# Feed-forward blocks as pairs of tiles across batches, behind an exact top-32 attention

## The chip, the cores and the metric

The kernel runs on one core of a Trainium2 chip, in one launch. The metric is device time in microseconds (us). A core has five engines that run their own instruction streams in order: TensorE (PE, matmuls; its weight loads are listed apart as PEld), VectorE (DVE), ScalarE (ACT), GpSimd (POOL) and SyncE (SP), which here only issues DMAs.

## The reference

Eight batches, eight heads, 576 positions, head dimension 64; then a feed-forward part over all 4608 positions with 512 inputs, 2048 hidden units and 512 outputs.

```python
scores = q @ k.T / sqrt(64)                       # per batch and head, 576 x 576
kth    = np.partition(scores, -32)[..., -32]      # the 32nd largest of each row
scores = np.where(scores >= kth, scores, -1e9)
attn   = softmax(scores)
x      = (attn @ v), heads side by side           # (4608, 512)
h      = x @ w_in                                 # (4608, 2048)
g      = np.where(h > 0, h, exp(min(h, 0)) - 1)   # ELU
out    = g @ w_out                                # (4608, 512)
```

All is in float32. The two weight matrices arrive as float64 and are decoded on the chip during the first steps.

## The kernel before

**Steps.** A batch has four query tiles of 128 rows (numbers 0 to 3) and a remainder of 64 rows (number 4, `J` in the code). The heads are taken in pairs. One step is one query tile and one head pair: 128 rows x 576 keys, twice. Two remainders share a step: it takes four heads of 64 rows. So a batch has 4 x 4 + 2 = 18 steps, and the whole kernel 144. The list `steps` fixes their order. Before, batch 0 takes its tiles one by one and then the remainder; every other even batch takes tiles (0,1), then (2,3), then the remainder; an odd batch begins with the remainder and goes on with (0,1) and (2,3). Inside a group such as (0,1) the order is head pair by head pair, and for each head pair tile 0 and then tile 1.

**What a step does.** `scores` (L329) is four fp32 matmuls of 288 columns on PE (eight half-high ones in a remainder step), and ACT copies and scales them (L337). In the profile each fp32 matmul of the program is two instructions. `select` (L349 to L363) finds the 32nd largest value of every row on DVE with four MAX8 and three MATCH_REPLACE8 for each of the two heads: it is almost all of DVE's work. `mask` (L382 to L386) does mask and exponential on ACT. `normalise` (L396 to L403) divides on POOL. `turn` (L422, L423) transposes the weights of the step on PE in nine chunks of 128 and copies them to `et` with ACT. `attend` (L448) multiplies by v, once per group and head pair: 20 matmul instructions of 256 columns for a group of two tiles, 20 of 128 columns for a single tile, and 40 of 64 columns for a remainder step. `finish` (L475) copies the result into `xT`, the input of the feed-forward block to which the tile belongs.

**The order on PE.** Every engine's instructions stay in the order in which the main loop at the end of the kernel writes them. Iteration n writes: the scores of step n+2, the attend of a group that became complete, then four quarters. The selection of step n is spread over the quarters on DVE; mask and normalise are those of step n-1, and the transposes are those of step n-2. At the end of each quarter `feed` may put feed-forward pieces in. `todo` holds loads and transposes of the next batch's k and q, and loads of v, at steps given by `plan`: `load_halves` issues eight DMAs on SP, `start_qk` leads to two transposes on DVE (L283), `load_v` issues four DMAs on SP and two memsets on POOL. A buffer of `kqT` or `vT` (five each) comes free after the last scores or the last attend that use it.

**Feed-forward blocks.** A `Block` holds one, two or three tiles (`slots`). It becomes ready when the attends of all its tiles are done. Then `ffn_pieces` makes 16 hidden pieces and, per tile, four projection pieces. A hidden piece (L523) is four matmuls (eight instructions) of 128 x `slots` columns; ACT makes ReLU twice and an exponential (L533, L536, L538) and mostly a subtraction (L542), and POOL (L493) or DVE (L495) adds the halves. A projection piece (L551) is four matmuls (eight instructions) of 512 columns for one tile. A tile is stored from `osb` by SP.

Before, the first two batches form five single blocks and two pairs; each further two batches form the blocks (0,1), (2,3), (remainders, 0, 1 of the odd batch) and (2,3 of the odd batch): three pairs and a triple. In all there are five singles, eleven pairs and three triples for 36 tiles.

**The planner.** `HIDDEN` and `PROJECT` give each piece a planned cost; a single has 31.8 units in all, a pair 58.0, a triple 85.8. The list `due` holds for each block the step at which it becomes ready and the units of all blocks that were ready before it. `feed` goes on at the lowest rate that any of these due times asks for:

```python
ahead = [(w - fed["sum"]) / (x - fed["at"]) for x, w in due if x > fed["at"]]
if ahead:
    fed["over"] += max(0.0, share * min(ahead))
```

So the work that is at hand is spread up to the next block that is late in coming. Some entries of `due` before: 391.0 units at step 66.5, 650.8 at 102.5, 910.6 at 138.5, 996.4 at 146.5; the sum of all blocks is 1054.4. Pieces that are left when the loop ends are written behind it.

Of the kernel before, what the change touches and what calls it, by code (L numbers as in the profile page):

```python
# [10 lines left out]
FP32 = mybir.dt.float32  # L11
# [5 lines left out]
TAKEN = -1.0e30  # L17
EPS = 1.0e-9
STEEP = 2.0**96
HIDDEN = {1: 1.1, 2: 1.85, 3: 2.7}  # L20
PROJECT = 3.55


# [57 lines left out]
def kernel(  # L81
# [10 lines left out]
    P = nc.NUM_PARTITIONS  # L92
    B, H, S, D = q.shape
    dm, dff = moe_w_in.shape[0], moe_w_in.shape[1] // 2
    J = S // P
    JP = J * P
    R = S - JP
# [2 lines left out]
    NC = dm // P  # L100
    NF = dff // P
    NG = NF // 2
    T = 3 * P
    KEYS, QUERIES = R, R + S
    Q = 32
    NB = S // Q
# [19 lines left out]
    late = {}  # L126
# [342 lines left out]
    def finish(blk, parts, at, cols, src):  # L469
        if blk.xT is None:  # L470
            if blk.slots == 1:
                blk.xT = xpool.tile([P, NC, P], FP32, tag="xT", name="xT")
            else:
                blk.xT = late["x"].tile([P, NC, T], FP32, tag="xT", name="xT")
        nc.scalar.copy(blk.xT[:, at, cols], src)  # L475
# [7 lines left out]
    def close_gates(keep=0, upto=None):  # L483

        while gates:
            put, group, dst, n, apart = gates[0]
            if put > place[0] - keep if upto is None else group > upto:
                return  # L490
            gates.pop(0)
            if apart:
                nc.gpsimd.tensor_tensor(dst, n, dst, ALU.add)  # L493
                continue
            nc.vector.scalar_tensor_tensor(  # L495
                out=dst, in0=n, scalar=-1.0, in1=dst, op0=ALU.add, op1=ALU.add
            )

    def ffn_pieces(blk):
        n_tok = blk.slots * P  # L500
        bank = dm // n_tok
        unit = max(2, bank)

        def hidden(f):
            if f == 0 and blk.number == 0:
                g = early.tile([P, NF, P], FP32, tag="g", name="gT")
                blk.gT = [g[:, 0:NG], g[:, NG:NF]]
            elif f % NG == 0 and blk.number > 0:
                g = late["g"].tile([P, NG, T], FP32, tag="g", name="gT")
                blk.gT.append(g[:])  # L510
            if f % unit == 0:
                if len(gates) > 1:
                    close_gates(upto=gates[0][1])
                if blk.number == 0:
                    n = earlyf.tile([P, 4 * P], FP32, tag="n", name="n")
                else:
                    n = late["f"].tile([P, 2 * T], FP32, tag="n", name="n")
                blk.n = n[:, 0 : unit * n_tok].rearrange("p (f t) -> p f t", f=unit)
            if f % bank == 0:
                ps = ps_f.tile([P, dm], FP32, tag="f", name="hps")  # L520
                blk.h = ps[:, 0 : bank * n_tok].rearrange("p (f t) -> p f t", f=bank)
            for i in range(NC):
                nc.tensor.matmul(  # L523
                    blk.h[:, f % bank, :],
                    w_in[:, i, f * P : (f + 1) * P],
                    blk.xT[:, i, 0:n_tok],
                    start=(i == 0),
                    stop=(i == NC - 1),
                )
            g, end = blk.gT[f // NG], f % NG + 1  # L530
            if end % bank == 0:
                n0 = f % unit + 1 - bank
                nc.scalar.activation(  # L533
                    blk.n[:, n0 : n0 + bank, :], blk.h, AF.Relu, scale=-1.0
                )
                nc.scalar.activation(g[:, end - bank : end, 0:n_tok], blk.h, AF.Relu)  # L536
            if end % unit == 0:
                nc.scalar.activation(blk.n, blk.n, AF.Exp, scale=-1.0)  # L538
                dst = g[:, end - unit : end, 0:n_tok]
                apart = place[0] > 4 * (tight + 3) and blk is not blocks[-1]  # L540
                if apart:
                    nc.scalar.activation(blk.n, blk.n, AF.Copy, bias=-1.0)  # L542
                gates.append((place[0], (blk.number, f + 1 - unit), dst, blk.n, apart))

        def project(s, part):
            close_gates(upto=(blk.number, (part + 1) * NF // 4 - 1))
            if part == 0:
                blk.o = ps_f.tile([P, dm], FP32, tag="f", name="ops")
            step = NF // 4
            for f in range(part * step, (part + 1) * step):  # L550
                nc.tensor.matmul(  # L551
                    blk.o[:],
                    blk.gT[f // NG][:, f % NG, s * P : (s + 1) * P],
                    w_out[:, f, :],
                    start=(f == 0),
                    stop=(f == NF - 1),
                )
            if part == 3:
                o = opool.tile([P, dm], FP32, tag="osb", name="osb")
                nc.scalar.copy(o[:], blk.o[:])  # L560
                for t in blk.tiles[s]:
                    p0 = t.cols.start - s * P
                    nc.sync.dma_start(out[t.rows, :], o[p0 : p0 + t.ql, :])

        part = HIDDEN[blk.slots]
        behind = 2 * NF if blk.number else 0
        return [
            (part, max(behind, NC * (f // 4 + 1)), lambda f=f: hidden(f), blk.number)
            for f in range(NF)
        ] + [  # L570
            (PROJECT, max(behind, NF + (part + 1) * NF // 4),
             lambda s=s, part=part: project(s, part), blk.number)
            for s in range(blk.slots)
            for part in range(4)
        ]

    ffn = []
    steps, first, due = [], {}, []
    blocks, tight = [], 2 * NHP
    for b in range(B):  # L580
        if b % 2 == 0:
            rest = 2 * J
            division = [(0,), (1,), (2,), (3,), (rest,), (4, 5), (6, 7)]
            if b > 0:
                division = [(0, 1), (2, 3), (rest, 4, 5), (6, 7)]
            slots = {}
            for part in division:
                blk = Block(len(blocks), len(part))
                blocks.append(blk)
                slots.update((x, (blk, s)) for s, x in enumerate(part))  # L590
        first[b] = len(steps)
        tiles = []
        for qt in range(J + 1):
            r0 = b * S + (JP if qt == J else qt if b == 0 else qt * P)
            if qt == J:
                (blk, slot), c0, n = slots[rest], (b % 2) * R, R
                rows = slice(r0, r0 + R)
            else:
                (blk, slot), c0, n = slots[(b % 2) * J + qt], 0, P
                rows = slice(r0, r0 + J * (P - 1) + 1, J) if b == 0 else slice(r0, r0 + P)  # L600
            c0 += slot * P
            t = Tile(b, qt, rows, blk, slice(c0, c0 + n))
            blk.left += NHP
            blk.tiles[slot].append(t)
            tiles.append(t)
        order = [(0, 1), (2, 3), (J,)] if b % 2 == 0 else [(J,), (0, 1), (2, 3)]
        if b == 0:
            order[:2] = [(0,), (1,), (2,), (3,)]
        for qts in order:
            for hp in range(NHP // 2 if qts == (J,) else NHP):  # L610
                group = Group([tiles[qt] for qt in qts], hp)
                steps += [Step(tiles[qt], hp, group, i) for i, qt in enumerate(qts)]
            for qt in qts:
                n = len(steps)
                tiles[qt].block.ready = n + 2.0 if n <= tight else n + 2.5
    NS = len(steps)
    total = 0.0
    for blk in sorted(blocks, key=lambda x: x.ready):
        due.append((blk.ready, total))
        total += NF * HIDDEN[blk.slots] + 4 * blk.slots * PROJECT  # L620

    todo = {}

    def at(step, fn, *args):
        todo.setdefault(step, []).append((fn, args))

    for b in range(1, B):
        f = first[b]
        plan = ((7, 5, 2), (5, 3, -2), (3, 1, -2), (1, -1, -3))
        if b % 2 == 1:  # L630
            plan = ((7, 5, 0), (6, 4, -2), (5, 3, -3), (4, 3, -3))
        for hp, (ahead, ready, late_v) in enumerate(plan):
            at(f - ahead, load_halves, b, hp)
            at(f - ready, start_qk, b, hp)
            at(f - late_v, load_v, b, hp)
# [44 lines left out]
    main, rest, other = slice(0, J), slice(J, J + 1), slice(J + 1, 2 * J + 1)  # L680
# [69 lines left out]
```

## Time and profile before

| | |
|---|---|
| time, median of 3 runs | 1633.8 us (1633.7 to 1633.95) |
| the profiled execution's own time | 1633.17 us |
| its span | 1631.4 us |
| granted TensorE clock, mean | 0.988 |
| PE, matmuls | 1569.5 us busy, 8276 instructions |
| PEld, weight loads | 1004.7 us |
| DVE | 1454.4 us, 2980 instructions |
| ACT | 1174.6 us |
| POOL | 711.6 us |
| hidden matmuls, L523 | 2432 instructions: 1408 of 256 columns, 384 of 384, 640 of 128 |
| projection matmuls, L551 | 1152 instructions of 512 columns |

The span runs from the first to the last instruction; 1.8 us of the profiled execution lie around it. Busy times of engines overlap, so they say which engine is loaded, not what the end waits for. Matmul ends are modelled in the profile, and matmuls overlap: the time that a group of matmuls takes from PE is read from its start to the start of the next group, not from its own length.

### The profile page before, as it was taken

The page shows a single profiled execution, that of the slowest core. Times are in us where ns is not written, and L with a number is a line of the kernel's source. Part 1 is how long each engine was busy: PE and PEld are TensorE (multiplying, and loading weights), DVE is VectorE, ACT ScalarE, POOL GpSimd, SP SyncE. Part 2 cuts the span into 40 slices and gives each one's busy share as a digit, 9 for nine tenths or more (in the row PEclk, how much of TensorE's full clock was granted, in tenths as well). Part 3 has the DMA queues.
Part 4 walks back from the last instruction along what each step waited for, and adds up shares of the span by engine and source line. Part 5 has one row for each costly group of instructions (what it writes and reads, how often), then busy time and mean ns, then how long its engine had stood idle before and what let it go on. Part 6 is the DMA issues. An engine that isn't in the chain of part 4 may idle for free.

```text
span 1631.4 us, 25301 instructions
## 1 busy us (share of the span) xinstructions
PE 1569.5 (96%) x8276; PEld 1004.7 (62%) x8276; DVE 1454.4 (89%) x2980; ACT 1174.6 (72%) x2369; POOL 711.6 (44%) x1535
## 2 busy tenths in 40 slices
PE   4789999999999999999999999999999999999999
PEld 2477666766665757555566666655557575755564
DVE  7899999999999999999999699999999599998000
ACT  6987777877776868778577786868668695958521
POOL 4983345444443444444344443535435353534300
PEclk9779999999999999999999999999999999999999
DMA  8521310012100310022000200012100201000000
GB/s 243 187 79 36 65 37 1 7 22 45 43 1 19 54 37 7 7 40 46 23 8 15 55 21 25 1 28 45 36 14 1 43 1 36 1 13 1 7 14 13
DMA packets 188035, 56.17 MB, mean 34 GB/s; under 512 B 178176, under 2 KB 179200, under 8 KB 187904
## 3 DMA queue, kind: packets, MB, share of 16 engines
q1 hardware_dynamic: 186704, 54.26, 14.1%
q8 instruction: 66, 1.08, 0.3%
q14 instruction: 65, 0.53, 0.1%
q10 hardware_dynamic: 1200, 0.30, 0.1%
HBM read 45.09 MB, written 9.44 MB: 33 GB/s over the span
## 4 chain that ended last, share of the span: by engine, by line
PE 74%; ACT 14%; DVE 5%; POOL 3%; issue 1%; SPq 1%; DMA 1%; ACTq 0%; DVEq 0%; POOLq 0%
PE ops L551 29%; PE hps L523 22%; PE avps L448 10%; PE scps L329 7%; PE eps L422 5%; ACT sc L386 3%; DVE wk L356 2%; ACT sc L385 2%; ACT et L423 2%; DVE m L363 2%; ACT n L542 1%; ACT n L533 1%; ACT n L538 1%; ACT gT L536 1%; POOL sc L403 1%
## 5 line engine op out<-in xcount | busy, mean ns | idle before, releaser
L363 DVE MAX8 m<-wk 128x8 f32<-128x576 f32 x864 | 611.2, 751 | 0.3 <-POOL den L384 0.3
L523 PE MATMUL hps<-xT,w_in 128*128 128x256 f32 (+2 forms) x2432 | 542.9, 373 | 0.0
L551 PE MATMUL ops<-w_out,gT 128*128 128x512 f32 x1152 | 522.5, 598 | 0.0
L523 PEld LDWEIGHTS hps<-xT,w_in 128*128 128x128 f32 x2432 | 404.9, 192 | 97.4 <-issue 25.4
L356 DVE MATCH_REPLACE8 wk<-m,wk 128x576 f32<-128x576 f32 x576 | 424.5, 747 | 0.0
L551 PEld LDWEIGHTS ops<-w_out,gT 128*128 128x128 f32 x1152 | 208.6, 190 | 231.7 <-issue 230.6
L396 POOL TENSOR_SCALAR dene<-den 128x2 f32<-128x2 f32 x144 | 32.5, 225 | 693.1 <-ACT sc L386 692.5
L386 ACT ACTIVATE sc<-sc,den 128x576 f32<-128x576 f32 x288 | 223.4, 776 | 66.1 <-POOL den L384 44.4
L385 ACT ACTIVATE sc<-sc,m 128x576 f32<-128x576 f32 x288 | 225.0, 781 | 9.6 <-DVE m L363 9.5
L337 ACT ACTIVATE sc<-scps 128x576 f32<-128x576 f32 x288 | 170.9, 646 | 77.8 <-PE scps L329 77.8
L448 PE MATMUL avps<-et,vT 128*64 128x256 f32 (+2 forms) x2080 | 205.6, 328 | 20.1 <-ACT et L423 19.7
L329 PE MATMUL scps<-kqT 64*128 64x288 f32 (+1 forms) x1280 | 199.9, 443 | 25.1 <-ACT kqT L305 12.6
L349 DVE MAX8 m<-sc 128x8 f32<-128x576 f32 x288 | 202.6, 747 | 20.6 <-ACT sc L337 20.6
L403 POOL TENSOR_SCALAR sc<-sc,rec 128x576 f32<-128x576 f32 x288 | 213.5, 751 | 14.9
L423 ACT COPY et<-eps 128x512 f32<-128x512 f32 x288 | 164.6, 571 | 66.2 <-PE eps L422 66.2
L356 DVE MATCH_REPLACE8 wk<-m,sc 128x576 f32<-128x576 f32 x288 | 212.2, 746 | 0.0
L448 PEld LDWEIGHTS avps<-et,vT 128*64 128x64 f32 x2080 | 128.0, 141 | 101.0 <-ACT et L423 34.2
L422 PEld LDWEIGHTS eps<-ident,sc 128*128 128x128 f32 x1152 | 143.4, 143 | 72.4 <-issue 53.9
L493 POOL TENSOR_TENSOR gT<-n,gT 128x512 f32<-128x512 f32 (+1 forms) x120 | 166.2, 1385 | 38.0 <-ACT n L542 38.0
L422 PE MATMUL eps<-ident,sc 128*128 128x128 f32 x1152 | 174.1, 277 | 0.1
L329 PEld LDWEIGHTS scps<-kqT 64*128 64x128 f32 (+1 forms) x1280 | 107.0, 182 | 102.5 <-issue 46.2
L533 ACT ACTIVATE n<-hps 128x512 f32<-128x512 f32 (+1 forms) x156 | 87.0, 558 | 58.0 <-PE hps L523 57.1
(45 smaller groups left out, 988.5 us busy)
## 6 DMA issues: line engine op xcount, KB each, us to landing
raw<-in_moe_w_in_dram SPq DMA_DIRECT2D x16, 512.0 KB, 4.9
vT<-in_v_dram SPq DMA_DIRECT2D x64, 128.0 KB, 2.4
raw<-in_moe_w_out_dram SPq DMA_DIRECT2D x16, 512.0 KB, 3.8
out_dram<-osb SPq DMA_DIRECT2D x32, 256.0 KB, 2.0
kin<-in_k_dram SPq DMA_DIRECT2D x112, 72.0 KB, 2.4
qin<-in_q_dram SPq DMA_DIRECT2D x112, 72.0 KB, 2.5
kin<-in_k_dram SPq DMA_DIRECT2D x8, 128.0 KB, 4.7
vT<-in_v_dram SPq DMA_DIRECT2D x64, 16.0 KB, 2.2
```

Source lines behind the costliest of these rows:

```text
L329: nc.tensor.matmul(wide[i][rows, half, 0:HS], kq[part, q0 : q0 + u.t.ql], kq[part, k0 : k0 + HS], start=True, stop=True,)
L349: nc.vector.max(found[i], cur[i])
L356: nc.vector.match_replace(wk[i], found[i], cur[i], TAKEN)
L363: nc.vector.max(found[i], cur[i])
L385: nc.scalar.activation(sc, sc, AF.Prelu, scale=-1.0, bias=low, alpha=1.0 / STEEP)
L386: nc.scalar.activation(sc, sc, AF.Exp, scale=-STEEP, bias=gap, accum_out=u.den[:, i : i + 1])
L403: nc.gpsimd.tensor_scalar(u.sc[:, i, :], u.sc[:, i, :], rec[:, i : i + 1], 1.0, ALU.mult, ALU.mult)
L422: nc.tensor.transpose(ps[:, c * P : (c + 1) * P], sc[:, c0 : c0 + P], ident[:])
L423: nc.scalar.copy(g.et[:, chunks, u.at, :], ps[:, 0 : n * P].rearrange("p (c q) -> p c q", c=n),)
L448: nc.tensor.matmul(ps[i * D : (i + 1) * D, cols], vt[:, 2 * J + i if c == J else i * J + c, :], w, start=(c == 0), stop=(c == J),)
L523: nc.tensor.matmul(blk.h[:, f % bank, :], w_in[:, i, f * P : (f + 1) * P], blk.xT[:, i, 0:n_tok], start=(i == 0), stop=(i == NC - 1),)
L551: nc.tensor.matmul(blk.o[:], blk.gT[f // NG][:, f % NG, s * P : (s + 1) * P], w_out[:, f, :], start=(f == 0), stop=(f == NF - 1),)
```

## The change

The blocks are no longer cut inside two batches. The list `ends` holds all tiles in the order in which they become complete (a pair of remainders counts where the odd batch's remainder stands), and is cut into five blocks of one tile and then blocks of two; the last tile is left over as a single block. So that two tiles of a pair come together, a batch whose first tile would complete a pair takes its tiles as (0), (1,2), (3) in place of (0,1), (2,3): these are batches 3, 4 and 7. There are now six singles and fifteen pairs. The largest block has two tiles, so `T` falls from 384 to 256, and with it the sizes of `xT`, `gT` and `n`. A further plan holds for an even batch that begins with one tile (batch 4). Entries of `due` are now 391.0 units at step 62.5 and then 58 more every 8 steps up to 971.0 at 142.5, and 1029.0 at 146.5; the sum is 1060.8.

```diff
-HIDDEN = {1: 1.1, 2: 1.85, 3: 2.7}
+HIDDEN = {1: 1.1, 2: 1.85}
...
-    T = 3 * P
+    T = 2 * P
...
-                    n = late["f"].tile([P, 2 * T], FP32, tag="n", name="n")
+                    n = late["f"].tile([P, 4 * P], FP32, tag="n", name="n")
...
+    orders, ends, division = [], [], []
     for b in range(B):
-        if b % 2 == 0:
-            rest = 2 * J
-            division = [(0,), (1,), (2,), (3,), (rest,), (4, 5), (6, 7)]
-            if b > 0:
-                division = [(0, 1), (2, 3), (rest, 4, 5), (6, 7)]
-            slots = {}
-            for part in division:
-                blk = Block(len(blocks), len(part))
-                blocks.append(blk)
-                slots.update((x, (blk, s)) for s, x in enumerate(part))
+        if b == 0:
+            order = [(0,), (1,), (2,), (3,)]
+        elif (len(ends) + b % 2 - J - 1) % 2 == 0:
+            order = [(0, 1), (2, 3)]
+        else:
+            order = [(0,), (1, 2), (3,)]
+        orders.append([(J,)] + order if b % 2 else order + [(J,)])
+        ends += [(b, qt) for qts in orders[b] for qt in qts if qt < J or b % 2]
+    while ends:
+        n = 1 if len(blocks) <= J else 2
+        blk = Block(len(blocks), len(ends[:n]))
+        blocks.append(blk)
+        division += [(x, (blk, s)) for s, x in enumerate(ends[:n])]
+        del ends[:n]
+    slots = dict(division)
+    for b in range(B):
         first[b] = len(steps)
         tiles = []
         for qt in range(J + 1):
             r0 = b * S + (JP if qt == J else qt if b == 0 else qt * P)
             if qt == J:
-                (blk, slot), c0, n = slots[rest], (b % 2) * R, R
+                (blk, slot), c0, n = slots[b | 1, J], (b % 2) * R, R
...
-                (blk, slot), c0, n = slots[(b % 2) * J + qt], 0, P
+                (blk, slot), c0, n = slots[b, qt], 0, P
...
-        order = [(0, 1), (2, 3), (J,)] if b % 2 == 0 else [(J,), (0, 1), (2, 3)]
-        if b == 0:
-            order[:2] = [(0,), (1,), (2,), (3,)]
-        for qts in order:
+        for qts in orders[b]:
             for hp in range(NHP // 2 if qts == (J,) else NHP):
...
         plan = ((7, 5, 2), (5, 3, -2), (3, 1, -2), (1, -1, -3))
+        if len(orders[b][0]) == 1:
+            plan = ((7, 5, 2), (5, 3, 0), (3, 1, -1), (2, 0, -2))
         if b % 2 == 1:
             plan = ((7, 5, 0), (6, 4, -2), (5, 3, -3), (4, 3, -3))
```

Each entry of `plan` is for one head pair: how many steps before the batch's first step its k and q are loaded, its transposes begin and its v is loaded (a negative number lies behind the first step).

## Prediction

> **What bounds the kernel now.** I read the page first: TensorE is the busiest engine, VectorE the next, and the slices show where each gives out.
>
> ```profile
> PE 1569.5 (96%) x8276; PEld 1004.7 (62%) x8276; DVE 1454.4 (89%) x2980; ACT 1174.6 (72%) x2369; POOL 711.6 (44%) x1535
> PE   4789999999999999999999999999999999999999
> DVE  7899999999999999999999699999999599998000
> ```
>
> PE is full from the fourth slice on; DVE is full until about slice 22, then dips, and has nothing to do in the last three slices, where only feed-forward matmuls are left. A PE that is "9" everywhere can still wait, because its ends are modelled. So I cut the span at three starts of score matmuls in the timeline of PE: the scores of step 32 start at 329.8, of step 72 at 739.2, of step 140 at 1457.9, and PE's last matmul ends at 1627.6. The table of stages (columns: busy time of each engine):
>
> ```profile
> 329.80:739.20 409.40, 401.12 (x2081) 256.88 (x2080) 406.73 (x837) 306.84 (x618) 179.35 (x410) 1.00 0.14 28
> 739.20:1457.90 718.70, 715.78 (x3661) 446.29 (x3660) 680.86 (x1402) 531.14 (x1074) 312.50 (x708) 1.00 0.11 23
> 1457.90:1627.60 169.70, 168.65 (x629) 98.29 (x628) 53.86 (x108) 79.02 (x156) 39.21 (x75) 1.00 0.03 8
> ```
>
> In stage A (40 steps, 10.24 us each) DVE is busy 406.7 of 409.4 us: DVE sets the pace. In stage B (68 steps, 10.57 us each) PE is busy 715.8 of 718.7 and DVE has 38 us of idle: PE sets the pace. Stage C is PE alone. To see PE's real need I price each kind of matmul by the start of its group to the start of the next group, in the timeline of PE:
>
> ```profile
> 134.01 1.31 PE L448 MATMUL avps<-et,vT 128*64 128x128 f32 x20
> 135.25 3.70 PE L551 MATMUL ops<-w_out,gT 128*128 128x512 f32 x8
> 138.79 0.60 PE L422 MATMUL eps<-ident,sc 128*128 128x128 f32 x4
> ...
> 168.77 1.06 PE L523 MATMUL hps<-xT,w_in 128*128 128x128 f32 x8
> 169.66 0.60 PE L422 MATMUL eps<-ident,sc 128*128 128x128 f32 x4
> ...
> 726.02 2.75 PE L523 MATMUL hps<-xT,w_in 128*128 128x384 f32 x8
> 728.60 0.60 PE L422 MATMUL eps<-ident,sc 128*128 128x128 f32 x4
> ...
> 1079.66 2.38 PE L448 MATMUL avps<-et,vT 128*64 128x256 f32 x20
> 1081.97 3.70 PE L551 MATMUL ops<-w_out,gT 128*128 128x512 f32 x8
> ...
> 1572.30 27.79 PE L523 MATMUL hps<-xT,w_in 128*128 128x256 f32 x128
> 1599.93 27.63 PE L551 MATMUL ops<-w_out,gT 128*128 128x512 f32 x64
> ```
>
> Prices: projection (512 columns) 0.43 us each (3.44 for 8 in undisturbed groups); hidden 128 columns 0.111 (0.89 for 8), 256 columns 0.217 (27.79 for 128), 384 columns 0.3225 (2.58 for 8); an attend of 256 columns 2.31, of 128 columns 1.24 (both 20 matmuls), of a remainder group 1.31; a transpose 0.109; the scores of a step 1.17. With the counts that stand between the same scores in the built program's order, stage A needs 264 x 0.43 + 512 x 0.217 + 72 x 0.3225 = 247.8 of feed-forward and 132.7 of attention, 380.5 together: 28.9 us of PE gap in 409.4. Stage B needs 470.2 + 225.7 = 695.9: gap 22.8 in 718.7, or 0.335 us a step. Stage C needs 141.3 + 24.1 = 165.4: gap 4.2. The waits of PE show what the gap in A is:
>
> ```profile
> PE avps L448 <- ACT et L423: 19.7, 26, 2.4
> ```
>
> Most of these lie before 800 us: PE runs ahead of a late DVE, and catches up with the last transposed chunk that ACT still has to copy.
>
> **What moves.** The planner feeds feed-forward work by due times. Before, the first nine blocks (391 of its units) are spread up to step 66.5, since a triple is then the next to be ready; after, the same 391 units are due by step 62.5. From there on both run at nearly the same rate (259.8 units in 36 steps, 7.22 a step; after 58 in 8, 7.25). At the end, before leaves a pair (58 units) behind the last due time, after a single (31.8). So work of about one tile moves from the tail to steps 32 to 72. The order of the two built programs says the same: by step 72 the new kernel has issued 28.6 us more of feed-forward matmuls, and the difference stays between 26 and 29.5 us until step 140.
>
> **What it costs PE in total.** Nine tiles leave triples: 384 hidden matmuls x 0.3225 = 123.8 us become 512 x 0.217 + 128 x 0.111 = 125.3: +1.5. In three batches twelve paired attends become 24 single ones: 24 x 1.24 - 12 x 2.31 = +2.0. Projections, scores and transposes keep their number. Sum +3.5 us.
>
> A rule speaks against this. The Trainium skill, "TensorE: Matmul & The Clock Gate", Part 3, The mechanism, states that a weight load overlaps running matmuls only where the row groups differ. The rows differ from it: a load for `hps` takes 0.190 us, yet hidden matmuls of 128 columns start every 0.111 us, so loads lie under matmuls of the same rows. By the page the 256 added hidden loads and 240 added attend loads would be exposed, 256 x 0.190 + 240 x 0.137 = 81 us, and the kernel would take about 1700 us.
>
> **The stages after.** A: 320 x 0.43 + 640 x 0.217 = 276.5 plus attention 133.0 = 409.5, up 29.0. That is above DVE's 406.7, so the stage becomes like B, where PE needs 10.23 a step and DVE 10.0. I take B's gap, 0.335 x 40 = 13.4: 422.9, against 409.4: **+13.5**. Bounds: the calmest steps of B (1206 to 1248 us, for one) show 0.7 us of gap in four steps, 0.175 a step, giving 7 and +7.1; if nothing of the 28.9 is filled, +29.0. B: 520 x 0.43 + 1136 x 0.217 = 470.1 plus 227.1 = 697.2, **+1.3**. C: 160 x 0.43 + 144 x 0.217 + 128 x 0.111 = 114.3 plus 24.4 = 138.7, against 165.4: **-26.7**. Sum -11.9.
>
> Beside PE, at no cost: ACT's feed-forward work per tile is 9.67 us in a triple (32 x 0.4845 + 8 x 0.846 + 8 x 0.843, over 3) and 9.78 in a pair (16 x 0.5915 + 8 x 0.632 + 8 x 0.630, over 2); twelve more copies of attends add 1.9 us; ACT has 188 us idle in B. If that cover failed it would be 1.9 us. POOL's additions become 32 x 1.277 for 24 x 1.819, 2.8 us less. Twelve more attends can each meet a late ACT copy: ten single ones between 127 and 213 us took 1.58 on average, 0.34 over 1.24, so 4 us at most; but in the new order nearly every attend has a feed-forward piece between it and the transposes it needs, where 24 of 60 had none in A and B. I take 0 and keep -6 (24 bare attends at the mean excess of 0.28 in B's paired ones) to +4.
>
> The new load plan touches batch 4 alone. One load of k and q (eight DMAs on SP), one pair of transposes on DVE and three loads of v (four DMAs on SP and two memsets on POOL each) come one to two steps earlier; their numbers stay. A load of v and its memsets wait for an attend of batch 3, at the nearest one step earlier in the order; behind them stand output stores on SP (one every 14 us at the densest) and the next normalise on POOL. Odd batches of before have the same spacing in B and cost PE nothing there: 0. The scores of the last two head pairs now come one step after their transposes (1.5 us a pair), where before left two or more; a lagging DVE would hold PE by those 1.5 us and a ScalarE copy, some 2 us, twice. No row shows it: -1 to +4, taken as 0, since a stage set by PE leaves DVE ahead.
>
> In the tail the new kernel still covers the last chain: some 65 us of matmuls stand between the last scores and the last transposes; two selections of 9.7 us on DVE, the mask (4 x 0.78 on ACT) and the normalise (about 3 us on POOL) need under 30.
>
> The profiled execution took 1633.17 (span 1631.4, and 1.8 around it), 0.6 under the median 1633.8. 1633.17 - 11.9 = 1621.3; on the median's scale **1621.9**.
>
> **Rivals.** 0.2%, 3.3 us, is about what a measurement here can tell from no change.
> (1) *ACT, not DVE, makes the gap.* Then A keeps 28.9 (+15.5 over my sum), and each of twelve new attends pays the worst bare excess seen, 0.98: +11.8. Net +15.4: **1649, slower**. Place: the attend waits of steps 32 to 72 and of batches 3, 4, 7. It decides from a gap of 0.63 us a step in A (25.3 us). For it: in A the chain of waits runs 23% through ACT and 69% through PE. Against: ACT has nearly the same load per step in A and B (7.7 and 7.8 us), and in B the chain is 95% PE and 4% ACT.
> (2) *The gap is latency that neither grows nor fills:* A 438.4, sum +3.6, **1637**, at the edge between no change and slower.
> (3) *Everything runs as in the calmest steps,* since bare attends are gone: A 416.5, B 709.1, C 142.9, sum -29.2, **1605**. Against: batch starts, with their transposes on DVE, cost B 3.5 and 4.5 us of gap in four steps, twice.
>
> **Chances.** My forecast 0.72; its bounds (A's gap at 7, attends at -6, up to +4 and +4) give 1609 to 1630. Rival 1 0.08, rival 2 0.10, rival 3 0.10. The range 1609 to 1638 takes in rival 2 and leaves out 1 and 3. Faster: 0.72 less 0.03 for its upper end, plus rival 3, is 0.79; no change 0.03 and half of rival 2, 0.08; slower the other half and rival 1, 0.13.
>
> **What would show it.** Right: the scores of steps 32 and 72 some 423 us apart instead of 409, with DVE idle there; steps 72 to 140 unchanged at 10.6; the end beginning with a run of 128 hidden matmuls of 128 columns (14.2 us) and 13.8 of projection; DVE ending some 10 us later than before. Wrong: gaps above 25 us in A, attends waiting on ACT in batches 3 and 4, or a PE wait for transposed keys at step 72.

## The result: 27 us slower; stages A and B lose 55 us, the tail gains 29

The changed kernel takes 1660.77 us (median of 4 runs, 1660.61 to 1661.11) against 1633.75 in the same session: ratio 1.0168, 95% interval 1.0150 to 1.0185. The prediction was 1621.9, with 1638 as its upper end and 0.13 for slower.

The page of the profile after, engines and slices:

```profile
PE 1572.4 (95%) x8772; PEld 1050.6 (63%) x8772; DVE 1453.2 (88%) x2976; ACT 1181.3 (71%) x2385; POOL 721.2 (43%) x1551
PE   4789999999999999999999999999999999999999
DVE  7899999999998899989898599989999779999500
```

The work is what was counted: 8772 matmul instructions are 256 hidden and 240 attend instructions more than 8276. PE looks full as before. But DVE now has dips from slice 13 on: its first operation of a step (L349) waited 55.9 us in all for ScalarE's scores, and 20.6 us in the kernel before. The stages are cut at the same scores as in the prediction (steps 32, 72, 140, end of PE):

```profile
331.60:763.30 431.70, 421.92 (x2233) 274.68 (x2232) 418.23 (x860) 315.45 (x635) 185.32 (x418) 1.00 0.14 28
763.30:1514.60 751.30, 724.31 (x3959) 480.14 (x3958) 677.42 (x1392) 540.18 (x1089) 316.49 (x713) 1.00 0.10 22
1514.60:1654.90 140.30, 140.30 (x677) 90.32 (x676) 43.47 (x87) 69.17 (x140) 38.76 (x79) 1.00 0.03 8
```

Stage A went from 409.4 to 431.7 us (the sum had 422.9), stage B from 718.7 to 751.3 (720.0), stage C from 169.7 to 140.3 (142.9). With 1.8 us lost before step 32 and 0.2 gained behind PE's last matmul that is +27.1, the difference of the spans. The tail did what was forecast, and stage B lost 31 us that the sum did not have. PE's waits in stage B, first of the kernel before and then of the changed one (total, times, longest):

```profile
PE avps L448 <- ACT et L423: 1.8, 2, 1.1
```

```profile
PE avps L448 <- ACT et L423: 27.0, 21, 2.8
```

So attends wait for ScalarE's copy to `et`. (This view counts idle time alone; from start to start, the measure of the table further below, stage B's attends lose 30 us more than before.) One of them, in the timeline of PE and then in that of ACT:

```profile
1311.76 0.60 PE L422 MATMUL eps<-ident,sc 128*128 128x128 f32 x4
1312.20 1.89 PE L523 MATMUL hps<-xT,w_in 128*128 128x256 f32 x8
1314.02 1.24 PE L329 MATMUL scps<-kqT 64*128 64x288 f32 x8
1315.19 0.65 PE L448 MATMUL avps<-et,vT 128*64 128x256 f32 x2
1316.80 2.37 PE L448 MATMUL avps<-et,vT 128*64 128x256 f32 x18 [0.96 <-ACT et L423]
```

```profile
1313.26 0.78 ACT L386 ACTIVATE sc<-sc,den 128x576 f32<-128x576 f32 x1
1313.94 0.19 ACT L386 ACTIVATION_READ_ACCUMULATOR sc<-sc,den 128x1 f32 x1
1314.03 0.58 ACT L533 ACTIVATE n<-hps 128x512 f32<-128x512 f32 x1
1314.51 0.59 ACT L536 ACTIVATE gT<-hps 128x512 f32<-128x512 f32 x1
1314.99 0.63 ACT L538 ACTIVATE n<-n 128x512 f32<-128x512 f32 x1
1315.65 0.63 ACT L542 ACTIVATE n<-n 128x512 f32<-128x512 f32 x1
1316.18 0.57 ACT L423 COPY et<-eps 128x512 f32<-128x512 f32 x1
```

PE goes on from the transposes at 1312.2. A hidden piece (1.82 us to the next start) and the scores (1.17) lie between them and the attend, so PE's side has its cover. The copy starts 4 us after the transposes, because four operations for a finished bank of hidden units (two ReLU, exponential, subtraction) stand ahead of it in ScalarE's queue. The attend's first two matmuls use an earlier copy and go; the other eighteen wait.

In the program order, an iteration has four quarters, and the last transposes with their copy stand between the third feed and the fourth. A pair's PSUM bank holds two hidden pieces, and a piece is fed about once a quarter; so banks end either in quarters 1 and 3 or in 2 and 4. A bank that ends in quarter 3 stands ahead of the copy, one in quarter 4 behind it. In stage B the kernel before ended 4, 29, 5 and 31 banks in quarters 1 to 4, the changed kernel 34, 2, 34 and 2 (a hidden piece of a triple fills a bank alone). Its plan repeats every 8 steps (58 units at 7.25 a step), so each block falls into the same phase.

### The profile page after: what moved, and what is told of

Same layout as the page of the kernel before. It is cut to its first block, busy times and chain, and to the rows that moved or that the text cites. A ratio compares the mean times of both kernels' runs of the same rounds, so it can differ in the third digit from the quotient of the medians.

```text
span 1658.5 us, 26360 instructions
## 1 busy us (share of the span) xinstructions
PE 1572.4 (95%) x8772; PEld 1050.6 (63%) x8772; DVE 1453.2 (88%) x2976; ACT 1181.3 (71%) x2385; POOL 721.2 (43%) x1551
## 4 chain that ended last, share of the span: by engine, by line
PE 66%; ACT 24%; DVE 7%; issue 1%; POOL 1%; DMA 0%; ACTq 0%; SPq 0%; DVEq 0%; POOLq 0%
PE ops L551 29%; PE hps L523 15%; PE avps L448 10%; PE scps L329 6%; ACT sc L386 5%; PE eps L422 5%; ACT sc L385 4%; DVE wk L356 3%; ACT n L542 3%; ACT et L423 3%; ACT n L533 3%; ACT n L538 3%; ACT gT L536 2%; DVE m L363 2%; ACT sc L337 1%
## 5 line engine op out<-in xcount | busy, mean ns | idle before, releaser
L523 PE MATMUL hps<-xT,w_in 128*128 128x256 f32 (+1 forms) x2688 | 547.7, 354 | 0.0
L523 PEld LDWEIGHTS hps<-xT,w_in 128*128 128x128 f32 x2688 | 444.0, 193 | 62.3 <-issue 20.8
L349 DVE MAX8 m<-sc 128x8 f32<-128x576 f32 x288 | 202.6, 745 | 56.8 <-ACT sc L337 55.9
L493 POOL TENSOR_TENSOR gT<-n,gT 128x512 f32<-128x512 f32 x136 | 173.6, 1277 | 145.9 <-ACT n L542 145.9
L448 PEld LDWEIGHTS avps<-et,vT 128*64 128x64 f32 x2320 | 136.2, 141 | 128.5 <-ACT et L423 61.9
L533 ACT ACTIVATE n<-hps 128x512 f32<-128x512 f32 x144 | 84.7, 588 | 85.2 <-PE hps L523 85.1
```

The source lines that it names most:

```text
L349: nc.vector.max(found[i], cur[i])
L448: nc.tensor.matmul(ps[i * D : (i + 1) * D, cols], vt[:, 2 * J + i if c == J else i * J + c, :], w, start=(c == 0), stop=(c == J),)
L523: nc.tensor.matmul(blk.h[:, f % bank, :], w_in[:, i, f * P : (f + 1) * P], blk.xT[:, i, 0:n_tok], start=(i == 0), stop=(i == NC - 1),)
```

## Experiments

Theory P (place of the bank in ScalarE's queue) stood against S (single-tile groups and their extra attends) and L (ScalarE overloaded while a pair's hidden pieces run). The kernel before took 1633.4 to 1633.7 us beside these runs.

**e1_due_quarter**

```diff
-                tiles[qt].block.ready = n + 2.0 if n <= tight else n + 2.5
+                tiles[qt].block.ready = n + 2.0 if n <= tight else n + 2.75
```

> The changed kernel, with one constant of the planner altered: a block counts as ready 2.75 steps behind its last step and not 2.5. Work, groups and blocks stay; hidden pieces start one quarter of a step later, so a pair of them (one PSUM bank, four ScalarE operations of 2.45 us) ends in the second and fourth quarter and no longer in the first and third. Attends that come right behind a third-quarter bank fall from 32 to 2 in steps 32 to 140. Theory P (place of the bank: its four ScalarE operations stand before the last copy to et, and the attend waits for that copy): about 1.3 us saved for each of 30, so 1660.8 falls to some 1622 to 1632, and PE's wait on ACT et shrinks from 27 us to under 6 between the scores of steps 72 and 140. Theory S (the single-tile groups and their twelve more attends cost the time): stays at 1658 to 1662. Theory L (ScalarE has too much to do while a pair's hidden pieces run, wherever they stand): stays at 1655 to 1662.

Measured: 1618.48 us, ratio 0.9907 (0.9892 to 0.9922). It is 42 us faster than the changed kernel and a little below P's range. Stage A takes 417.8, stage B 714.0. PE's wait on `et` in B:

```profile
PE avps L448 <- ACT et L423: 1.1, 2, 1.0
```

One constant of the planner turns a loss of 27 us into a gain of 15, with the same work, groups and blocks. S and L fail: neither allows a gain.

**e2_turn_first**

```diff
         next(passes)
-        feed(n, 0.25)
         if done:
             turn(done, other)
+        feed(n, 0.25)
         next(passes)
```

> The changed kernel, with the last four transposes of a step and their copy to et written ahead of the third feed and not behind it. Banks still end in the first and third feed, but their ScalarE operations now stand behind the copy. Theory P: the waits go as in the shifted planner, 1622 to 1635. Theory S: 1658 to 1662. Theory L: 1655 to 1662, since ScalarE does the same work in the same step.

Measured: 1606.31 us, ratio 0.9832 (0.9817 to 0.9847). Below P's range again: the size of P's saving was underestimated, its sign was right. Stages A and B take 1131.5 us together, as in e1 (1131.8); the 12 us between the two runs are the tail, 140.3 against 151.4.

**e3_before_due_quarter** (the constant of e1 in the kernel before)

> The kernel before, with the same constant 2.75: pairs and triples as before, no single-tile groups. Attends right behind a third-quarter bank rise from 9 to 17 in steps 32 to 140. Theory P: 8 x 1.3 us, slower by 7 to 13 us, 1641 to 1647. Theory S and theory L: 1632 to 1636.

Measured: 1656.42 us, ratio 1.0137 (1.0120 to 1.0154). The kernel before, with triples and no single groups, becomes nearly as slow as the changed one when its banks move to quarter 3. P's size was too small: 8 x 1.3 was expected and 22.7 came. Stage B took 24.0 us more, 19.9 of it attends; the later due time also left the tail 4.4 us longer, and A was 4.9 us shorter.

**e4_pairs_no_singles**

```diff
-            order = [(0,), (1, 2), (3,)]
+            order = [(0, 1), (2, 3)]
...
-        late["x"] = ctx.enter_context(tc.tile_pool(name="xt", bufs=2))
+        late["x"] = ctx.enter_context(tc.tile_pool(name="xt", bufs=3))
```

> The changed blocks (pairs across batches) with every later batch in tile order (0,1),(2,3), so that no single-tile groups remain; xT has three buffers and not two, since a group can feed two blocks. Hidden pieces stand in mixed quarters: 13 attends behind a third-quarter bank against 32. Theory P: 19 x 1.3 us less, 1632 to 1640. Theory S: all of the loss goes, 1618 to 1626. Theory L: 1655 to 1662.

Measured: 1642.85 us, ratio 1.0059 (1.0044 to 1.0074), 3 us above P's range and far from S and L. Alone this run would leave P and S open, because it changes both the groups and the place of the banks; e8, 20.5 us faster with the same groups, separates them.

**e5_before_turn_first** (the edit of e2 in the kernel before)

> The kernel before, with the last four transposes ahead of the third feed. It has 9 attends behind a third-quarter bank in steps 32 to 140, and 7.7 us of attend waits between the scores of steps 72 and 140. Theory P: a small gain, some 6 us there and up to 3 us before it, where VectorE sets the pace: 1622 to 1630. Theory S, with any effect of the edit apart from the place of banks: the same 54 us gain that the changed kernel had from this edit, about 1580. With it the changed kernel under the same edit (1606.3) shows what pairs are worth when the place of banks plays no part; the prediction's sum for that was 11.9 us.

Measured: 1620.79 us, ratio 0.9922 (0.9907 to 0.9936), 1 us under P's range. So the kernel before lost 13 us in the same way, and with that loss removed from both the change is worth 1620.8 - 1606.3 = 14.5 us, where the prediction's sum had 11.9. By stages, from e5 to e2: A 404.1 to 418.0, B 716.2 to 713.6, C 167.2 to 140.3, or +13.9, -2.6 and -26.9, where the sum had +13.5, +1.3 and -26.7.

**e6_both_edits** (e1 and e2 together)

> The changed kernel with both edits: ready 2.75 and the last transposes first. The copy to et is then ahead of every bank that ends in quarters two and four as well. Theory P: both edits remove the same waits, so they do not add up: 1603 to 1612. If they act on different things they add up: about 1564.

Measured: 1612.80 us, ratio 0.9872 (0.9857 to 0.9887). One microsecond over P's range; the edits do not add up. It is slower than e2 alone: A and B take 1129.8 against 1131.5, but the tail takes 147.9 against 140.3: by count 3.5 us of matmuls more are left to it, and its attends wait some 4 us.

**e7_due_half** (the constant of e1 at 3.0)

> The changed kernel with ready 3.0, so that hidden pieces start two quarters later than in the changed kernel, and banks end in the first and third quarter again: 34 attends stand behind a third-quarter bank, 32 in the changed kernel. Theory P: as slow as the changed kernel, 1655 to 1668. If a later due time in itself saved the time: below 1620.

Measured: 1668.07 us, ratio 1.0210 (1.0195 to 1.0225), at P's upper end. A later due time is no cure; it is the quarter that counts.

**e8_pairs_turn_first** (e4 and e2 together)

> The changed blocks without single-tile groups (tile order (0,1),(2,3) everywhere, three buffers for xT), with the last transposes first. Against the changed kernel with that edit (1606.3) it shows what the single-tile groups cost when no attend waits: by the prediction 2.0 us of matmuls, so 1602 to 1606; theory S: 10 us or more less, under 1597.

Measured: 1622.32 us, ratio 0.9929 (0.9913 to 0.9946): neither range. Without single-tile groups the kernel is 16 us slower, not faster. The end of its timeline of PE says why:

```profile
1533.71 27.79 PE L523 MATMUL hps<-xT,w_in 128*128 128x256 f32 x128
1561.34 27.63 PE L551 MATMUL ops<-w_out,gT 128*128 128x512 f32 x64
1588.80 14.45 PE L523 MATMUL hps<-xT,w_in 128*128 128x128 f32 x128
1603.10 13.90 PE L551 MATMUL ops<-w_out,gT 128*128 128x512 f32 x32
```

With the group (2,3) last, the last pair and the last single become ready together, and three tiles are left for the tail, which takes 168.9 us against 140.3 in e2. The order (0), (1,2), (3) is what leaves one. Stages A and B take 404.5 and 715.5 here (418.0 and 713.6 in e2), so the work that left the tail in the changed kernel never entered A.

**e9_copy_before_bank** (ScalarE's queue alone)

```diff
+            def bank_done(h=blk.h, n=blk.n):
...
+                    gates.append((place[0], (blk.number, f + 1 - unit), dst, n, apart))
+            if hold[0]:
+                held.append(bank_done)
+            else:
+                bank_done()
...
         next(passes)
+        hold[0] = n > tight + 3 and done is not None
         feed(n, 0.25)
         if done:
             turn(done, other)
+        hold[0] = False
+        while held:
+            held.pop(0)()
         next(passes)
```

> The changed kernel with one edit on ScalarE alone: the four operations of a bank that ends in the third quarter are issued behind the copy to et of that quarter and not ahead of it. The orders on TensorE and VectorE are those of the changed kernel, instruction for instruction; 54 copies to et move past a bank. It tells the queue of ScalarE apart from where TensorE's transposes and hidden matmuls stand, which the two earlier edits moved as well. Theory P: the 50 us that attends wait behind third-quarter banks fall under 12 us, and the kernel takes 1606 to 1622. If the place of the matmuls on TensorE mattered instead: 1650 or more.

Measured: 1606.64 us, ratio 0.9840 (0.9825 to 0.9854). PE's and DVE's orders are those of the changed kernel, and 54 us are gone, 49 of them attend excess in A and B. The timeline of ACT, and of PE, at the same kind of place (line numbers of this run's kernel are shifted: its L536 is L533 of the changed kernel, its L524 is L523):

```profile
1268.31 0.78 ACT L386 ACTIVATE sc<-sc,den 128x576 f32<-128x576 f32 x1
1268.99 0.19 ACT L386 ACTIVATION_READ_ACCUMULATOR sc<-sc,den 128x1 f32 x1
1269.09 0.56 ACT L423 COPY et<-eps 128x512 f32<-128x512 f32 x1
1269.55 0.60 ACT L536 ACTIVATE n<-hps 128x512 f32<-128x512 f32 x1
```

```profile
1266.81 0.60 PE L422 MATMUL eps<-ident,sc 128*128 128x128 f32 x4
1267.25 1.89 PE L524 MATMUL hps<-xT,w_in 128*128 128x256 f32 x8
1269.07 1.24 PE L329 MATMUL scps<-kqT 64*128 64x288 f32 x8
1270.24 2.38 PE L448 MATMUL avps<-et,vT 128*64 128x256 f32 x20
```

The same PE order as above runs through: the copy ends 0.6 us before the attend begins, and the bank's operations run under the attend. PE's busy time now fills both stages; how much it still waits, the counted needs tell further below:

```profile
329.10:747.20 418.10, 417.76 (x2235) 273.46 (x2234) 414.99 (x854) 314.97 (x635) 184.96 (x419) 1.00 0.14 27
747.20:1460.90 713.70, 712.79 (x3957) 477.42 (x3956) 676.38 (x1393) 537.99 (x1090) 315.40 (x713) 1.00 0.11 23
```

**e10_quarter_and_turn** (e2 with the constant at 2.25)

> The changed kernel with the last transposes first and ready 2.25, one quarter of a step earlier. Theory P: no third-quarter bank is left, as with the transposes first alone (1606.3): 1602 to 1613. A small gain over it is possible if work reaches TensorE earlier.

Measured: 1612.78 us, ratio 0.9875 (0.9859 to 0.9892), inside P's range and no gain over e2.

The runs side by side. "Behind a bank" counts attends of steps 32 to 139 that follow a third-quarter bank in the program order (of e9, where the copy passes the bank, none; the expectations have 32, 2 and 17 where the table has 31, 1 and 18); the excess sums, over all attends of these steps, the time from the attend's start to PE's next group less the undisturbed price (2.31, 1.24 or 1.31 us).

| kernel | behind a bank, of all | attend excess, us | time, us |
|---|---|---|---|
| before | 9 of 60 | 21.5 | 1633.8 |
| changed | 31 of 70 | 51.6 | 1660.8 |
| e1, 2.75 | 1 of 70 | 7.7 | 1618.5 |
| e2, transposes first | 0 of 70 | 2.6 | 1606.3 |
| e3, before, 2.75 | 18 of 60 | 39.1 | 1656.4 |
| e4, no singles | 13 of 60 | 30.3 | 1642.9 |
| e5, before, transposes first | 0 of 60 | 12.7 | 1620.8 |
| e6, 2.75, transposes first | 0 of 70 | 7 | 1612.8 |
| e7, 3.0 | 34 of 70 | 49.7 | 1668.1 |
| e8, no singles, transposes first | 0 of 60 | 11 | 1622.3 |
| e9, copy first | 0 of 70 | 2.5 | 1606.6 |
| e10, 2.25, transposes first | 0 of 70 | 8 | 1612.8 |

In the changed kernel the 31 attends behind a bank cost 50.1 of the 51.6 us, 1.6 us each; the other 39 cost 1.5 us together.

## Why the prediction was wrong

**The step that failed** is the one on extra attends: "nearly every attend has a feed-forward piece between it and the transposes it needs ... I take 0 and keep -6 ... to +4." Measured: +30 us of attend excess, all of it in B, where 22 of the 31 attends behind a bank stand; in A the excess is some 14 us in both kernels, more than the whole gap of 13.4 us that the sum left there. The cover was looked for in PE's order alone. The same feed-forward piece that covers the wait on PE puts four operations into ScalarE's queue, and in quarter 3 they come ahead of the copy. ScalarE's load (7.7 us in a step of 10) was weighed, its order was not, though the built programs showed it; counting attends behind a third-quarter bank would have given 31 where before had 9.

**A line was read too widely.** The prediction gives 19.7 us of attend waits as "what the gap in A is"; that is the whole run. The same view of stage A alone, first of the kernel before and then of the changed one:

```profile
PE avps L448 <- ACT et L423: 6.4, 9, 2.4
```

```profile
PE avps L448 <- ACT et L423: 9.4, 8, 1.5
```

Of the 19.7 us, 10.6 lie before step 32 and 1.8 in B. The waits that were in A did not shrink when the work moved there.

**Stage B's +1.3** went with it. The sum took B's gap over from the kernel before, 0.335 us a step. That gap was no property of PE work at this rate; it held because before's banks ended in quarters 2 and 4. The gap became 751.3 - 697.2 = 54.1, and 30.0 of the 31.3 us more are attends. One of their waits was followed by a slower clock: behind 2.8 us of idle PE at 996 us the granted clock was 0.50 from 1000.3 to 1003.7, and the 16 projection matmuls there took 8.7 us from start to start, where 16 take 7.0 in the tail.

**Stage A's +13.5** became +22.3: its gap fell from 28.9 to 22.2 and not to 13.4. Nine attends behind a bank take 13.6 us of the 22.2. In e9, without them, the gap is 418.1 - 409.5 = 8.6, near the calm end that the prediction named (7).

**Right:** the work that moves and where to, the cost of narrower matmuls (e9's stages fit the counted 409.5 and 697.2 with gaps of 8.6 and 16.5), the end (128 hidden matmuls in 14.3 us and 13.9 of projection), the new load plan at no visible price (no wait of PE for transposed keys is listed in A or B). The end to end saving that was argued for is there once the queue is in order: 14.5 us between e5 and e2. That A's share comes out, +13.9 for +13.5, is in part luck: A's gap goes from 23.6 (e5) to 8.5 (e2), where the sum went from 28.9 to 13.4, both ends some 5 us too high. DVE is busy 415.0 of the 418.1 us of stage A in e9, so the two engines are nearly level there, and the runs do not say which of them sets that pace.

**The rivals.** Rival 1 named the right wait, ACT's copies, with 1649. Its cause was not the one found: it had twelve new attends paying 0.98 each and A's gap staying, where 31 attends, old and new, paid 1.6, most of them in B. Rival 2 fell, since A's gap is 8.6 us in e9 and not 28.9. Rival 3, 1605 with every step as calm as the calmest, is what e2 and e9 reach, with an edit that the forecast kernel did not have.

**The rule on weight loads** that the prediction cites from the Trainium skill ("TensorE: Matmul & The Clock Gate", Part 3, The mechanism: a load overlaps running matmuls only where the row groups differ) does not hold in these runs either; the same section also lets a load go ahead into a background weight buffer. The changed program has 496 more loads, hidden matmuls of 128 columns still start every 0.112 us in the tail (14.3 us for 128) with loads of 0.19 us, and with the copies in order the kernel with more loads is the faster one.

**Left open:** why e7 is 7 us slower than the changed kernel with nearly the same count of late copies. Its stage A takes 8 us more, B 10 us less and the tail 7 us more, and 2.5 us are lost before step 32. By count 5 of the tail's 7 us are matmuls that moved there; the rest was not tried further.

## What to carry to other kernels

A piece of work that hides a wait on one engine also puts its own follow-up work into the queues of the others. Before calling a wait covered, list what stands ahead of the releasing instruction in its own engine's order, and not only what stands ahead of the waiting one. Where a planner feeds work by due times, a change of rate or block size shifts the phase of that work against fixed points of the loop: write urgent copies ahead of the feed, so that the phase matters little (e2, e6 and e10 lie within 7 us), before judging the change itself.

## What the runs showed that I had not expected

The phase alone, one constant of the planner (2.5 or 2.75), was worth 42 us of 1660 in one kernel and 23 us the other way in the other; the change under study cost 27. And the change, which lost 1.7% as it stood, beats the kernel before by 1.6% with 54 copies moved ahead of ScalarE's bank operations (e9, 0.9840) or with four transposes written a few lines earlier (e2, 0.9832). Against the kernel before with the same four transposes moved (e5) the gain is 14.5 us, 0.9%.
